# Nine score rounds for four groups of heads, with the diagonal's squares in tiles of their own, and a written list of steps

## The chip, the cores and the metric

The kernel runs on one core of one Trainium2 chip, as one launch. The metric is the device time of that launch in microseconds (us); lower is better. Five engines work side by side and are synchronised by semaphores: TensorE (PE, with its weight loads as PEld), VectorE (DVE), ScalarE (ACT), GpSimd (POOL) and SyncE (SP), which here only issues DMAs.

## The reference

Two layers, each an attention with a compressive memory and then a ReLU feed-forward, on x of 2048 tokens by 640 in bfloat16. The same weights serve both layers. The sequence is cut into N = 4 segments of L = 512 tokens; there are H = 32 heads of Dh = 20.

```python
def _A_ref(x, wq, wk, wv, wo, beta):
    q, k, v = ...                       # x @ wq, wk, wv; by head and segment
    phi = lambda t: jnp.where(t > 0, t + 1.0, jnp.exp(t))
    mask = (ar[:, None] < ar[None, :]) * -1e9
    for s in range(N):
        logits = jnp.einsum('bhqd,bhkd->bhqk', qs, ks) * scale + mask
        a_dot = jnp.einsum('bhqk,bhkd->bhqd', softmax(logits), vs)
        pq = phi(qs)
        num = jnp.einsum('bhld,bhde->bhle', pq, M)
        den = jnp.einsum('bhld,bhd->bhl', pq, z)[..., None] + 1e-06
        o = g * (num / den) + (1.0 - g) * a_dot
        pk = phi(ks)
        M = M + jnp.einsum('bhld,bhle->bhde', pk, vs)
        z = z + jnp.einsum('bhld->bhd', pk)
    return o @ wo
# twice: x = x + A(layernorm(x)); x = x + relu(layernorm(x) @ w1) @ w2
```

Attention is causal inside a segment, so of the 512 by 512 scores of a head and segment only the lower triangle counts.

## The kernel before, in words

x stays in SBUF for the whole run (`x_sb`, 16 tiles of 128 tokens). For each layer and segment the kernel normalises 512 tokens, transposes them, multiplies by wk, wq and wv, spills k and q to a DRAM scratch and reads them back into a padded layout (`pad`, four buffers, each for two groups of four heads): head hh of a group lies on the partitions 32 hh to 32 hh + 19. A score matmul therefore uses 20 rows of a 32-row strip of TensorE, and the four heads of a group run on the four strips side by side ("row tiles", 32 by 128).

**Score rounds.** `scores` (L1279 on) walks over 32 pairs of groups m (16 for each layer, four for each segment) and, for each, over the five rounds u of `ROUNDS` (L1274). An entry (z, j, o) of a round is: group z of the pair, key tile j of 128 keys, against the queries from 128 j to the end of the segment, written from column o. Key tile 0 alone is 512 columns, tiles 1 and 3 together 384 + 128, the tiles 2 of both groups 256 + 256, so each round fills 512 columns for each of four heads. A round's two halves (k = 0 and 1, two heads each) take the two score slots of PSUM, X and Y, of two banks each; in the first half of the first segment a third slot Z is lent. `exps` (L1345) runs one exponential on ScalarE for each half (L1365, 128 partitions by 1024) into `PT`, where a group has 1280 columns for each head; `causal` (L1371) zeroes the upper triangle of each 128 by 128 block on the diagonal with GpSimd (L1377). `apply` (L1385, matmuls at L1397) multiplies the probabilities by v: v's 21 columns (20 and one of ones, for the sum) are the weights, one head on each of the four 32-column strips ("quarter" or column tiles, 128 by 32), and the 512, 384, 256 and 128 queries of the four key tiles stream through in four steps. Two groups of 64 (`BY_TOKEN`) are applied the other way round (L1436). The result is evicted (L1407), transposed by DMA, divided (L1491), joined with the memory's part (`mem_read`, L1180; the memory is updated by `mem_write`, L1238), multiplied by wo and added to x (L1519); the feed-forward's second product is added at L1614, and finished tiles are stored.

**Two forms of a matmul.** `group` (L759 on) can issue each matmul of 128 by 128 weights either whole (L774, "full") or as four matmuls of 32 weight columns each on the four column tiles (L777, "quarter"), with the same result. Which is taken is decided step by step.

**What sets the order.** Every part above is a Python generator (`scores`, `exps`, `apply`, `proj_one`, `ffn`, ...) that yields operations. `Sched.run` collects the next operation of each, works out start and end from planned costs, the granted semaphores and a table of shifts (`SHIFT`), and records the best one, instruction after instruction, for every engine. A full or quarter form follows from the last form used and from how soon an apply is due (`_mode`). The engines then run these fixed programs; nothing is decided on the chip.

Of the kernel before, what the change touches and what calls it, by code (L numbers as in the profile page):

```python
# [5 lines left out]
dt = mybir.dt  # L6
# [27 lines left out]
PTH = 1280  # L34
BY_TOKEN = range(6,8)
PT_OFF = [0, 512, 1024, 896]
# [73 lines left out]
class Op:  # L110

    def __init__(self, alts, waits, dma=None, acq=None, urgent=False, take=(), mode="full", lag=0.0, port=False):
        self.lag = lag
# [8 lines left out]
        self.urgent = urgent  # L125
        self.take = take
        self.data = 0.0
# [32 lines left out]
class Spawn:  # L160
    def __init__(self, prio, gen):
        self.prio = prio
        self.gen = gen


LONE_NS = 300.0
SWITCH_NS = 96.0
COLS_LAG = 1500.0
SOFT = 400
SOFT_DMA = 1000  # L170
SOFT_FROM = ("sc",6,4,1)
SEM_NS = 60.0
PE_MARGIN = 80.0
HOLDERS = 1
SHIFT = {
# [41 lines left out]
}  # L217
HOLD_TOL = {"pe": 220.0, "act": 150.0, "dve": 200.0, "pool": 0.0, "sp": 0.0}


class Sched:


    def __init__(self, prog):
        self.P = prog
        self.free = {e: 800.0 for e in ENGS}
        self.t = {}
        self.events = {}
        self.streams = []
        self.dma_free = 0.0  # L230
        self.rank = {}
        self.mode = "full"
        self.soon = 0.0
        self.landed = set()
        self.met = {}
        self.seen = {}
        self.phase = {}
        self.made = {}
        self.held = {"dve": [], "pool": []}

    def add(self, prio, gen):
        self.streams.append([prio, gen, None, None, False])
        self.rank[id(gen)] = 0
# [8 lines left out]
    def enter(self, gen, phase):  # L252
        if self.phase.get(id(gen)) != phase:
            self.phase[id(gen)] = phase
            self.made[id(gen)] = 0

    def place(self, n, gen):
        k = self.made.get(id(gen), 0)
        return n, self.phase.get(id(gen), 0), sum(k >= x for x in (6, 20, 60))

# [6 lines left out]
    def _fill(self, st):  # L267
        while st[2] is None and not st[4]:
            try:
                y = next(st[1]) if st[3] is None else st[1].send(st[3][0])  # L270
            except StopIteration:
                st[4] = True
                return
            st[3] = None
            st[2] = y

    def _settle(self, st):

        while True:
            self._fill(st)  # L280
            if st[4]:
                return False
            y = st[2]
            if isinstance(y, (Op, Either)):
                return True
            if isinstance(y, Spawn):
                self.add(y.prio, y.gen)
                self.rank[id(y.gen)] = self.rank[id(st[1])]
                st[2], st[3] = None, (None,)
            elif isinstance(y, Need):  # L290
                if y.key not in self.events:
                    return False
                st[2], st[3] = None, (self.events[y.key],)
            else:
                s = self._pick(y.slots)
                if s is None:
                    return False
                s.free = False
                st[2], st[3] = None, (s,)
# [5 lines left out]
    def _mode(self, op):  # L305
        if op.cols is None:
            return op.mode
# [1437 lines left out]
```

## Time and profile before

| | |
|---|---|
| median of 3 runs (range) | 550.99 us (550.4 to 551.45) |
| span of the profiled execution | 549.3 us |
| the profiled execution's own time | not told apart among the three runs |
| TensorE busy | 539.8 us, 98% of the span, 9025 matmuls |
| VectorE busy | 427.8 us, 78% |
| ScalarE busy | 406.0 us, 74% |
| GpSimd busy | 195.7 us, 36% |
| exponentials (L1365) | 320, 308.9 us |
| score matmuls (L1301) | 1024, 63.4 us |

The span goes from the first to the last instruction of one profiled execution. Busy time is the time in which at least one instruction of that engine (or of that group) runs. A line number belongs to the kernel file; a line such as L774 can stand for many uses of one helper. `128*32` after a matmul's names is the size of its weights, rows by columns.

### The profile page before, as it was taken

Reading aid. Unit: us, or ns where it says so; the run is one execution under the profiler, and the core shown is the slowest. Engines: PE = TensorE matmul, PEld = TensorE weight load, DVE = VectorE, ACT = ScalarE, POOL = GpSimd, SP = SyncE. Lnnn points to the kernel's source line nnn. Section 1 sums busy time; section 2 is a strip of 40 time slices with the busy share of each in tenths; the row PEclk is TensorE's granted clock in tenths of the full one; section 3 lists DMA queues with packets and bytes.
Section 4 is the critical chain, followed back from the end, with each engine's and each line's share of the span. In section 5 each row is a group of like instructions: output and inputs, shape, how many; then the busy total and the mean of one; then the engine's idle time right before and its main releaser. Section 6 shows DMA issues by size and latency. Waiting matters only on the chain.

```text
span 549.3 us, 20483 instructions
## 1 busy us (share of the span) xinstructions
PE 539.8 (98%) x9025; PEld 305.5 (56%) x9025; DVE 427.8 (78%) x1067; ACT 406.0 (74%) x516; POOL 195.7 (36%) x305
## 2 busy tenths in 40 slices
PE   7999999999999999999999999999999999999997
PEld 6543464455554546646556555564646654757656
DVE  4899999898999989898778858997899788417102
ACT  5699899789888987788888867897778787350130
POOL 5255444333453334443433423433333333201000
PEclk9999999999999999999999999999999999999999
DMA  8699979715384175438384743336246511541201
GB/s 270 165 198 253 245 158 223 221 44 116 89 165 98 40 180 77 75 68 120 47 212 93 116 116 93 58 69 104 50 139 130 117 32 22 106 63 33 71 2 51
DMA packets 133325, 62.20 MB, mean 113 GB/s; under 512 B 112116, under 2 KB 123124, under 8 KB 133236
## 3 DMA queue, kind: packets, MB, share of 16 engines
q1 hardware_dynamic: 132672, 60.36, 51.5%
q8 instruction: 71, 1.16, 0.9%
q10 hardware_dynamic: 564, 0.53, 0.4%
q14 instruction: 18, 0.15, 0.1%
HBM read 20.56 MB, written 12.85 MB: 61 GB/s over the span
## 4 chain that ended last, share of the span: by engine, by line
PE 88%; ACT 6%; DVE 2%; DMA 2%; SPq 1%; issue 0%
PE ps L774 35%; PE ps L777 35%; PE ps L1301 8%; PE ps L1397 6%; ACT PT L1365 5%; PE ps L1180 2%; DMA x_sb<-in_A_x_dram 1%; PE ps L1572 1%; PE ps L1238 1%; DMA pad<-scr 1%; SPq L602 1%; DVE xn_tok L841 0%; SPq L612 0%; DVE stats L795 0%; DVE x_sb L1614 0%; DVE o_sb L1491 0%
## 5 line engine op out<-in xcount | busy, mean ns | idle before, releaser
L1365 ACT ACTIVATE PT<-ps 128x1024 bf16<-128x1024 f32 x320 | 308.9, 1028 | 59.3 <-PE ps L1301 57.6
L1377 POOL TENSOR_SCALAR_AFFINE_SELECT PT<-PT 128x512 bf16<-128x512 bf16 x256 | 169.3, 679 | 241.1 <-ACT PT L1365 241.0
L777 PE MATMUL ps<-xnT,w_r 128*32 128x512 bf16 x1256 | 76.0, 379 | 0.0
L777 PE MATMUL ps<-w_r,hT 128*32 128x320 bf16 (+1 forms) x1764 | 67.8, 295 | 0.0
L1614 DVE TENSOR_TENSOR x_sb<-x_sb,ps 128x320 bf16<-128x320 bf16 (+1 forms) x65 | 30.7, 474 | 43.6 <-PE ps L777 38.7
L1301 PE MATMUL ps<-pad 20*128 20x512 bf16 (+3 forms) x1024 | 63.4, 301 | 1.2 <-ACT PT L1365 0.7
L774 PE MATMUL ps<-w_r,hT 128*128 128x320 bf16 x404 | 64.2, 300 | 0.0
L795 DVE BATCH_NORM_STATS2 stats<-x_sb 128x6 f32<-128x320 bf16 x124 | 55.0, 478 | 3.8 <-DMA x_sb<-in_A_x_dram 3.0
L777 PEld LDWEIGHTS ps<-w_r,hT 128*32 128x32 bf16 x1764 | 45.2, 97 | 12.6 <-issue 1.4
L1595 ACT ACTIVATE hT<-ps 128x512 bf16<-128x512 f32 x50 | 29.9, 599 | 29.0 <-PE ps L777 25.6
L774 PE MATMUL ps<-xnT,w_r 128*128 128x512 bf16 x206 | 50.8, 380 | 0.0
L774 PEld LDWEIGHTS ps<-w_r,hT 128*128 128x128 bf16 x404 | 37.6, 98 | 19.4 <-issue 4.9
L1301 PEld LDWEIGHTS ps<-pad 20*128 20x128 bf16 x1024 | 17.9, 92 | 52.9 <-issue 24.5
L777 PEld LDWEIGHTS ps<-xnT,w_r 128*32 128x32 bf16 x1256 | 31.6, 97 | 27.8 <-issue 2.0
L1519 DVE TENSOR_TENSOR x_sb<-x_sb,ps 128x320 bf16<-128x320 bf16 x64 | 29.7, 478 | 20.4 <-PE ps L777 16.0
L811 POOL TENSOR_TENSOR rstd<-lnU,mhalf 128x2 f32<-128x2 f32 (+2 forms) x27 | 21.1, 782 | 63.5 <-DVE lnU L807 60.4
L1407 DVE CAST otu<-ps 128x512 bf16<-128x512 f32 x52 | 35.6, 685 | 9.1 <-PE ps L1397 8.2
L1397 PE MATMUL ps<-PT,v_aug 128*21 128x128 bf16 (+3 forms) x896 | 40.3, 300 | 0.0
L1594 DVE TENSOR_SCALAR hT<-ps 128x512 bf16<-128x512 f32 x54 | 36.5, 681 | 1.7 <-PE ps L774 0.7
L1491 DVE TENSOR_TENSOR o_sb<-otk,rden 128x320 bf16<-128x320 bf16 x62 | 34.8, 588 | 0.5
L981 DVE CAST stg<-ps 128x512 bf16<-128x512 f32 (+1 forms) x37 | 24.7, 669 | 12.5 <-PE ps L774 6.3
L1146 ACT ACTIVATE stg<-stg 128x512 bf16<-128x512 bf16 x50 | 31.7, 635 | 2.0 <-DVE rtmp L1144 1.8
(118 smaller groups left out, 731.5 us busy)
## 6 DMA issues: line engine op xcount, KB each, us to landing
pad<-scr SPq DMA_DIRECT2D x124, 80.0 KB
scr<-stg SPq DMA_DIRECT2D x34, 256.0 KB, 2.5
out_dram<-x_sb SPq DMA_DIRECT2D x15, 160.0 KB, 1.9
w_r<-in_B_w_dram SPq DMA_DIRECT2D x10, 216.0 KB, 4.0
w_r<-in_B_w_dram SPq DMA_DIRECT2D x13, 160.0 KB, 2.8
x_sb<-in_A_x_dram SPq DMA_DIRECT2D x10, 160.0 KB, 3.2
scr<-w_r SPq DMA_DIRECT2D x5, 256.0 KB, 4.2
wv_r<-in_A_wv_dram SPq DMA_DIRECT2D x1, 800.0 KB, 9.7
```

What stands on the lines that cost most here:

```text
L774: return e.matmul(view(dst.ap, b), a, b, start=(k == 0), stop=(k == last))
L777: return e.matmul(view(dst.ap[rows], b), part, b, start=(k == 0), stop=(k == last))
L795: tk = yield dve(320, 1, lambda e, c2=c2: e.bn_stats(stats6[:, t, c2, :], x_sb[:, t, c2 * 320:(c2 + 1) * 320]), xt)
L1146: te = yield act(512, lambda e, q=q: e.activation(q, q, ACT.Exp), [tr] + p, psum=False)
L1301: fns.append([(lambda e, z=z, j=j, hh=hh, N=N, o=o, sl=sl, q=hh % 2: e.matmul(slot.ap[:, q, o:o + N], sl.ap[32 * hh:32 * hh + DH, z, 0, 12 ...
L1365: tx = yield act(1024, lambda e, dst=dst, src=src: e.activation(dst, src, ACT.Exp, scale=SCALE), sc + pw)
L1377: tm = yield pool(600.0, lambda e, reg=reg: e.affine_select(out=reg, in_=reg, pattern=[[0, 4], [1, 128]], compare_op=ALU.is_ge, fill=0.0, ...
L1397: fns.append((lambda e, OD, j=j, hh=hh: e.matmul(OD.ap[32 * hh:32 * hh + DH + 1, 128 * j:L], VAUG[vx(a, s)][:, j, 4 * g + hh, :], pt.ap[:, ...
L1407: te = yield evac(L, 1, lambda e: e.tensor_copy(dst, OD.ap), lambda e: e.activation(dst, OD.ap, ACT.Copy), [tk] + OTU[0].tks)
L1491: to = yield dve(320, 1, lambda e, z=z, dst=dst: e.tensor_tensor(dst, av[:, z, :, :, 0:DH], rd.ap[:, z].to_broadcast([128, NJ, 4, DH]), AL ...
L1594: th = yield evac(512, 1, lambda e: e.tensor_scalar(hT[:, dc, :], bk.ap[:, :], 0.0, None, ALU.max), lambda e: e.activation(hT[:, dc, :], b ...
L1614: ta = yield dve(n, 1, lambda e: e.tensor_tensor(x_sb[:, t, c0:c0 + n], x_sb[:, t, c0:c0 + n], bk.ap[:, 0:n], ALU.add), [tk], urgent=True)
```

## The change

Three things change together.

*The layout of tokens.* In the segments 1 to 3, x is loaded so that in each odd tile the two halves of 64 tokens change places (two DMAs of 64 partitions for each pair of tiles), and stored back the same way. Segment 0 stays as it was ("plain").

*Scores and probabilities.* In the segments 1 to 3, the key tiles keep all queries that need the whole tile or its first diagonal square: the last diagonal square of 64 by 64 of each tile, four for each head, is taken out. What is left of a group fills two rounds of 512 columns (`FULLS`), so a group's part of `PT` shrinks from 1280 to 1024 columns. The squares of four groups (two pairs m, an even and the next odd one) make one ninth round in tiles of 32 rows by 64 columns, four squares for each of 16 heads. Its scores stand on 64 partitions for each key half, so it takes four exponentials (64 partitions by 1024) in place of two; they go to a new tile `DG`, of which the half that has no keys is set to zero. The apply of such a group has nine steps instead of four (`SUMS` and `DIAG`), over the same 1280 columns. In the plain segments the five rounds stay, with tile 2's probabilities in `DG`. One of the four `pad` buffers is given up for the room.

*The order.* The planner's choice is taken out. `ORDER` lists, for the whole kernel, which generator moves next, and with 80 added, that it takes its other alternative: quarter form for a matmul, VectorE in place of ScalarE for an eviction. `run` reads this list. The score rounds stay 320 halves less 24. Smaller edits: the first warming matmuls write other PSUM banks, and the last tile's three pieces are stored in halves over two queues.

```diff
-PTH = 1280
+PTH = 1024
-PT_OFF = [0, 512, 1024, 896]
+PT_OFF = [0, 512, None, 896]
+FULLS = (((0, 64, 448), (3, 384, 64)), ((2, 320, 192), (1, 256, 256), (1, 128, 64)))
+DIAG = ((0, 0, 0), (0, 3, 448), (1, 2, 256), (1, 1, 192))
+SUMS = ((0, 0, 448, 64), (3, 448, 64, 384), (2, 512, 192, 320), (1, 704, 256, 256), (1, 960, 64, 128))
...
+ORDER = """
+36 35 37*2 35 36*2 37 21 36 21 35 37 21 37 26 21 37 26*3 36 21*3 22*3 21 37 22 28 26 28 26 28 21 28 21 28 23 68 23
...
+        for word in ORDER.split():
+            code, _, count = word.partition("*")
+            for _ in range(int(count or 1)):
+                n, other = int(code) % 80, int(code) >= 80
+                st = tops[n] if n < 40 else next(x for x in self.kids[id(tops[n - 40])] if not x[3])
+                self._record(st, st[1].fn() if isinstance(st[1], Either) else st[1], other)
...
-        NPAD, NXT, NXN, NPT = 4, 2, 2, 2
+        NPAD, NXT, NXN, NPT = 3, 2, 2, 2
...
+        DG = sb("DG", [128, 2, 4, 4 * 128])
...
         ROUNDS = (((0, 0, 0),), ((0, 1, 0), (0, 3, 384)), ((0, 2, 0), (1, 2, 256)),
                   ((1, 0, 0),), ((1, 1, 0), (1, 3, 384)))
+        def plain(m):
+            return m % (NSEG * G // 2) < G // 2
+        def rounds(m):
+            return [u for u in range(5) if plain(m) or u != 2 or m % 2 == 0]
+        def turn_of(m, u):
+            if plain(m):
+                return [(z, 0, 128 * j, 128, 128 * j, L - 128 * j, o) for z, j, o in ROUNDS[u]]
+            if u == 2:
+                return [(z, 64 * (j % 2), q0, 64, q0, 64, 128 * z + 64 * y) for z in range(4) for y, j, q0 in DIAG]
+            o = [0]
+            for j, q0, nq in FULLS[u % 3]:
+                o.append(o[-1] + nq)
+            return [(u // 3, 0, 128 * j, 128, q0, nq, o[y]) for y, (j, q0, nq) in enumerate(FULLS[u % 3])]
...
-                        tx = yield act(1024, lambda e, dst=dst, src=src: e.activation(dst, src, ACT.Exp, scale=SCALE),
-                                       sc + pw)
-                        bkp.release(tx)
+                            moves = [(DG[r, t].rearrange("p z (h x) -> p h z x", h=4)[:, hs],
+                                      bkp.ap[r].rearrange("p h (z x) -> p h z x", z=4)) for t, r in enumerate(SIDES)]
+                        for dst, src in moves:
+                            tx = yield act(1024 if len(moves) == 1 else 1180, lambda e, dst=dst, src=src: e.activation(
+                                dst, src, ACT.Exp, scale=SCALE), sc + pw)
+                            ex.append(tx)
+                        bkp.release(*ex[-len(moves):])
...
+            if plain(n // 2):
+                sums = [(j, lambda hh, j=j: probs(j, hh, 128 * j, L - 128 * j), 128 * j, L - 128 * j) for j in range(NJ)]
+            else:
+                sums = [(j, lambda hh, c0=c0, nq=nq: pt.ap[:, hh, c0:c0 + nq], q0, nq) for j, c0, nq, q0 in SUMS]
+                sums += [(j, lambda hh, j=j, y=y: DG[:, j % 2, n % 4, 128 * hh + 64 * y:128 * hh + 64 * y + 64], q0, 64)
+                         for y, j, q0 in DIAG]
...
-                        S.last = yield dma(("sp", "sp", "act")[hf], dout, 256 * n, lambda e, c0=c0, n=n: e.dma_start(
-                            out[0, t * 128:(t + 1) * 128, c0:c0 + n], x_sb[:, t, c0:c0 + n]), tks)
+                        for k in range(2):
+                            S.last = yield dma(("sp", "act")[k], dout, 128 * n, lambda e, k=k, c0=c0, n=n: e.dma_start(
+                                out[0, t * 128 + 64 - 64 * k:t * 128 + 128 - 64 * k, c0:c0 + n],
+                                x_sb[64 * k:64 * k + 64, t, c0:c0 + n]), tks)
```

In `turn_of`, a part is (group, first output partition, first key, keys, first query, queries, column). A square of a key half with j odd goes to the partitions 64 to 127.

More of the change, by code (lines that the diff above doesn't have):

```diff
@@ L110, with __init__ @@
 class Op:
-    def __init__(self, alts, waits, dma=None, acq=None, urgent=False, take=(), mode="full", lag=0.0, port=False):
-        self.lag = lag
+    def __init__(self, alts, waits, dma=None, acq=None, take=(), mode="full", port=False):
         self.port = port
@@ L454, in pe, with _times @@
-def pe(ns, fns, waits=(), acq=None, take=(), mode="full", lag=0.0):
-    return Op([("pe", ns, fns, 190.0)], waits, acq=acq, take=take, mode=mode, lag=lag)
+    def _times(self, op, k, waits):
+        e, hold, fns, tail = op.alts[k]
+        m = PE_MARGIN if e == "pe" else 0.0
+        if e == "pe" and op.mode == "cols" and op.cols_ns is not None:
+            hold = op.cols_ns
+        if e == "pe" and op.mode != self.mode:
+            hold = hold + SWITCH_NS
+        start = max([self.at(t) + SEM_NS + m for t in waits], default=0.0)
+        start = max(self.free[e], start)
+        if e == "dve" and op.port:
+            for a, b in self.held["pool"][-6:]:
+                if a <= start + 66.0 < b:
+                    hold = max(hold, b - start + op.data - 70.0)
+        if e == "pool":
+            for a, b in self.held["dve"][-6:]:
+                if a < start + hold and b > start:
+                    hold = hold + b - max(a, start)
+        return start, start + hold
@@ new lines, in run @@
+    def run(self):
+        tops = list(self.streams)
+        first = tops[0]
+        self._settle_all()
+        for word in ORDER.split():
[4 more added lines that the diff above has]
+                self._record(st, st[1].fn() if isinstance(st[1], Either) else st[1], other)
+                self._settle(st)
+                self._settle_all()
+                if isinstance(first[1], Either):
+                    first[1].fn()
+        assert not self.streams
@@ new lines, in _record @@
+    def _record(self, st, op, other):
+        k = int(other and len(op.alts) > 1)
+        e, _, fns, tail = op.alts[k]
+        if op.cols is not None:
+            op.mode = "cols" if other else "full"
+            fns = op.cols if other else fns
+        waits, slot = op.waits, None
+        for s in op.take:
+            s.free = False
+        if op.acq is not None:
+            slot = self._pick(op.acq)
+            slot.free = False
+            waits = waits + slot.tks
+            fns = [(lambda eng, fn=fn, slot=slot: fn(eng, slot), mark) for fn, mark in fns]
+        start, end = self._times(op, k, waits)
+        self.P.waits(e, waits)
+        self.free[e] = end
+        if e == "pe":
+            self.mode = op.mode
+        if e == "dve" and op.port:
+            self.held[e].append((end - op.data, end))
+        elif e == "pool":
+            self.held[e].append((start, end))
+        if op.dma is not None:
+            tk = self.P.dma(e, fns[0][0], op.dma)
+            self.dma_free = max(self.dma_free, start + 300.0) + tail[1]
+            self.t[(id(tk[0]), tk[1])] = max(self.dma_free, end) + tail[0]
+            if tail[2]:
+                self.free[e] = max(end, self.dma_free)
+            out = tk
+        else:
+            marks = []
+            for fn, mark in fns:
+                tk = self.P.op(e, fn, mark)
+                if tk is not None:
+                    self.t[(id(tk[0]), tk[1])] = end + tail
+                    marks.append(tk)
+            out = marks[0] if len(marks) == 1 else (marks or None)
+        st[1], st[2] = None, ((slot, out) if slot is not None else out,)
@@ L458, in either, with pe @@
+def pe(ns, fns, waits=(), acq=None, take=(), mode="full"):
+    return Op([("pe", ns, fns, 190.0)], waits, acq=acq, take=take, mode=mode)
 def either(op, cols, ns=None):
@@ L633, in x_pieces @@
             def x_pieces(s):
-                def one(t):
-                    return lambda e: e.dma_start(x_sb[:, t, :], xs[:, t, :])
-                return [("x%d%d" % (s, i), 163840, one(4 * s + i)) for i in range(4)]
+                return [("x%d%d" % (s, i), 163840, fn) for i in range(2) for fn in pair_loads(4 * s + 2 * i)]
             def rows(name, w, src, k):
@@ L933, in proj_ln @@
             if a == 0:
-                xw = [[("x10",)]] * 2 + [[("x11",)]] * 2 if s == 1 else [[("x%d%d" % (s, i),)] for i in range(NJ)]
+                xw = [[("x10",)]] * 2 + [[("x11",)]] * 2 if s == 1 else [[("x%d%d" % (s, i // 2),)] for i in range(NJ)]
             else:
@@ L1371, in causal, with flat, mask @@
+        def flat(m):
+            b = 2 * (m % 2)
+            return DG[:, :, b:b + 2].rearrange("p t z (y q) -> p t (z y) q", y=2)
+        MK = {}
         def causal(m):
+            def mask(reg, n, base, w):
+                return pool(600.0, lambda e: e.affine_select(
+                    out=reg, in_=reg, pattern=[[0, reg.shape[1]], [1, n]], compare_op=ALU.is_ge, fill=0.0, base=base,
+                    channel_multiplier=-1), w)
             mk = [[], []]
-            for u, parts in enumerate(ROUNDS):
+            last = []
+            for u in rounds(m):
@@ L1374, in causal @@
                 ex = yield Need("ex", m, u)
[L1375 to L1383 removed]
+                z = u // 3
@@ L1609, in ffn @@
             hrest = yield Need("hR", b, s)
-            sums = [[] for _ in range(NJ)]
             def residual(i, hf, bk, tk, c0, n):
@@ L1665, in items @@
-        def items(f, count):
-            def g():
-                for n in range(count):
-                    S.enter(me, 2 * NSEG * n // count)
-                    yield from f(n)
-            me = g()
-            return me
-        for f in (scores, exps):
-            me = []
-            me.append(f(me))
-            S.add(0, me[0])
-        S.add(1, items(causal, NSEG * G))
-        S.add(1, items(apply, 2 * NSEG * G))
-        S.add(1, each(free_v))
-        S.add(1, items(turn_pair, NSEG * G))
@@ L1696, in bass_interleave_layers__memory_aug_infini_attn__dense_activation_relu__prompt_kernel, with each @@
-        S.add(5, first_sums())
-        for t in range(TT // NSEG):
-            S.add(5, first_one(t))
-        S.add(5, first_ln_b())
-        S.add(5, each(proj_ln))
-        S.add(5, proj_first())
-        S.add(5, each(proj_one(0)))
-        S.add(5, each(proj_one(1)))
-        S.add(4, each(proj_v))
-        S.add(6, each(ffn))
-        S.add(5, each(ffn_rest))
-        S.add(6, each(store))
-        S.add(7, warm_pe())
-        S.add(7, consts())
-        S.add(8, loads())
-        S.add(8, late_loads())
+        def each(f):
+            for a, s in AS:
+                yield from f(a, s)
@@ new lines, in items @@
+        def items(f, count):
+            for n in range(count):
+                yield from f(n)
+        S.add(scores())
+        S.add(exps())
+        S.add(items(causal, NSEG * G))
+        S.add(items(apply, 2 * NSEG * G))
+        S.add(each(free_v))
+        S.add(items(turn_pair, NSEG * G))
+        S.add(items(divide, NSEG * G))
+        S.add(each(turn_o))
+        S.add(each(out_proj(0)))
+        S.add(each(out_proj(1)))
+        S.add(each(ln_b(0)))
+        S.add(each(ln_b(1)))
+        S.add(each(fill))
@@ L1712, in bass_interleave_layers__memory_aug_infini_attn__dense_activation_relu__prompt_kernel @@
+        S.add(each(proj_v))
+        S.add(each(ffn))
+        S.add(each(ffn_rest))
+        S.add(each(store))
+        S.add(warm_pe())
+        S.add(consts())
+        S.add(loads())
+        S.add(late_loads())
         S.run()
```

613 lines of the change are left out of this document (306 added, 307 removed), and 41 rows, old and new, of the table SHIFT.

## The prediction

> **What bounds the kernel now.** I read the page first, then the busy time by stretch, then TensorE's order of time in one steady stretch, because the first two say that only TensorE matters and the third gives its prices.
>
> ```profile
> span 549.3 us, 20483 instructions
> PE 539.8 (98%) x9025; PEld 305.5 (56%) x9025; DVE 427.8 (78%) x1067; ACT 406.0 (74%) x516; POOL 195.7 (36%) x305
> PEclk9999999999999999999999999999999999999999
> 0.00:65.00 65.00, 59.56 (x741) 32.58 (x741) 54.25 (x143) 52.35 (x77) 32.20 (x61) 1.00 0.92 228
> 65.00:520.00 455.00, 453.96 (x7580) 255.19 (x7584) 369.47 (x917) 347.05 (x428) 163.51 (x244) 1.00 0.50 102
> 520.00:546.30 26.30, 26.28 (x712) 17.74 (x700) 3.74 (x8) 6.57 (x11) 0.00 (x0) 1.00 0.08 26
> ```
>
> The columns of the last three rows are stretch, length, then busy time of PE, weight load, VectorE, ScalarE and GpSimd, the granted clock and the DMA share. TensorE is idle for 5.44 us of the first 65, for 1.04 us of the next 455, and for nothing after that; the clock is whole throughout. So the time can fall only by less TensorE work or by the 5.4 us at the start. The span is 549.3 us and the median of the runs 550.99 us: about 1.7 us lie around the span. I work on the span and add them.
>
> **Prices on TensorE.** In these rows the first number is a start; the difference of two starts is what a piece costs, since matmuls overlap their own latency.
>
> ```profile
> 200.05 0.59 PE L774 MATMUL ps<-xnT,w_r 128*128 128x512 bf16 x2
> 200.58 0.40 PE L1301 MATMUL ps<-pad 20*128 20x384 bf16 x8
> 200.90 0.72 PE L1397 MATMUL ps<-PT,v_aug 128*21 128x512 bf16 x16
> 201.45 0.82 PE L777 MATMUL ps<-xnT,w_r 128*32 128x512 bf16 x12
> 202.10 0.34 PE L1180 MATMUL ps<-BD,phs 128*32 128x147 bf16 x12
> 202.27 1.25 PE L777 MATMUL ps<-xnT,w_r 128*32 128x512 bf16 x20
> 203.46 0.40 PE L1301 MATMUL ps<-pad 20*128 20x512 bf16 x4
> 203.78 0.99 PE L774 MATMUL ps<-w_r,hT 128*128 128x320 bf16 x6
> ...
> 147.18 0.46 PE L1238 MATMUL ps<-v_aug,phk 128*32 128x147 bf16 x32
> 147.57 0.39 PE L1301 MATMUL ps<-pad 20*128 20x512 bf16 x4
> ...
> 276.09 0.40 PE L1301 MATMUL ps<-pad 20*128 20x384 bf16 x8
> 276.42 0.72 PE L1397 MATMUL ps<-PT,v_aug 128*21 128x512 bf16 x16
> ```
>
> Twelve quarter matmuls (L777, four side by side) of 512 columns take 201.45 to 202.10: 0.217 us for four, some 0.42 ns a column. Twenty take five times that, 1.08 us; the next start comes 1.19 us later, so going from quarters to a score round costs 0.11 us. The round of one part (203.46 to 203.78) costs 0.32 us: 0.217 of columns and 0.10 to leave the row tiles. A round of two parts (276.09 to 276.42) costs 0.33: 0.01 for the second part. Two full matmuls and the way into a round take 0.53 us, which is 2 x 0.216 + 0.10: full and quarter form cost the same. An apply of 1280 columns in four steps (L1397) takes 0.55 us; 0.217 for 512 columns in one step would make 0.543 for 1280, and the three further steps bring the rest: from this and the 0.01 us of the reading, about 0.004 us a step. Three steps of 147 columns (202.10 to 202.27) take 0.17 us, 0.06 each.
>
> **Part 1, the score rounds.** Counted in the order of instructions, 160 rounds become 148: in the segments 1 to 3 of both layers, four groups (a group is four heads) took ten rounds and take nine. Eight of the nine carry 512 columns; the ninth carries 64 squares of 64 columns, on eight tiles at once if the two column halves of the array work together: 8 x 64 = 512 columns of time. That is one round's columns less, 0.217 us, in each of twelve places. Against it, parts: 16 per four groups become 20 in the full rounds (two or three in each) and 8 pairs of squares, 12 more at 0.01 = 0.12 us. Net 12 x (0.217 - 0.12) = **1.2 us less**. No row shows a 32 by 64 tile. Bounds: at best the squares' own parts cost nothing (1.0 us better, 2.2 less); at worst the column halves take turns, 16 steps of 0.037 instead of 8, 12 x 0.30 = 3.6 us dearer, 2.4 more. I take the first value because the quarter tiles, which also share rows, run four abreast, and the 32 matmuls at 147.18 start within 0.39 us, 0.10 of it the switch: 9 ns each, so that issue doesn't keep 64 squares from 0.3 us either (64 x 9 would be 0.58, but those 32 hold eight of 147 columns).
>
> **Part 2, the switches.** Changes of tile shape between neighbours on TensorE fall from 322 to 308: twelve rounds fewer (24), ten more between full and quarter form. 14 x 0.10 = **1.4 us less**.
>
> **Part 3, the apply.** For 48 of the 62 applies that work by head, four steps become nine over the same 1280 columns: 48 x 5 x 0.004 = **1.0 us more**.
>
> **Part 4, quarter form.** The list runs 678 matmuls in full form where 1359 ran, and 7328 quarter matmuls in place of 4604. By the rows above this costs nothing. In the memory update (L1238) the quarter form also skips columns: 13 full matmuls of 147 columns (0.06 us each) become quarters of 42 and 63 (0.03): **0.4 us less**.
>
> Sum of TensorE's work: -1.2 - 1.4 + 1.0 - 0.4 = **-2.0 us**, bounds -3.0 and +1.6.
>
> **Part 5, the exponentials.**
>
> ```profile
> L1365 ACT ACTIVATE PT<-ps 128x1024 bf16<-128x1024 f32 x320 | 308.9, 1028 | 59.3 <-PE ps L1301 57.6
> 201.01 1.94 ACT L1365 ACTIVATE PT<-ps 128x1024 bf16<-128x1024 f32 x2 [0.33 <-PE ps L1301]
> 33.84 26.73 ACT L1365 ACTIVATE PT<-ps 128x1024 bf16<-128x1024 f32 x29
> ```
>
> There is no gain here: a square round needs four instructions of 64 partitions by 1024 in place of two of 128 by 1024, so there are still 320, and the time goes with the 1024. Both score slots stay taken until all four are done. After a normal round that is 0.43 us (200.58 to 201.01) + 1.94; after a square round 0.43 + four at 0.92 (29 in 26.73 us) + 0.11 = 4.2 us. By the prices above, the new list puts 4.5 to 5.4 us of other TensorE work behind each of the twelve square rounds and, as before, about 2.5 us behind the others. This cover holds: cost nothing. If it went, each 0.1 us on each exponential beyond 1.1 us would cost 12 x 0.4 us.
>
> **Part 6, the start.** From 33.84 us on, ScalarE does 29 exponentials without a break: there it, not TensorE, sets the pace, and much of the 5.44 us lies in it. The first twenty rounds keep their number and form; the list puts 37.7 us of TensorE work from the first to the twentieth where 36.0 stood. Work that fills idle time there is gone later: up to 1.7 us. I take **1.0 us less**, as other waits of the start are for weights and inputs, whose loads stay in their order. x's two early pairs now come as four DMAs of half the partitions, two more issues on SP, beside the same bytes.
>
> **Part 7, everything else.** VectorE has 17 copies fewer and six maxima more, ScalarE 11 instructions more, of some 830 us busy together; GpSimd has the same number of masks of the same 512 elements. Two fills of zeros (1024 words on VectorE, one a layer) stand in front of the first squares' masks; the exponentials of the square round cover them. One of four pad buffers goes.
>
> ```profile
> 60.76 4.43 DMA pad<-scr
> PE ps L1301 <- DMA pad<-scr: 0.4, 1, 0.4
> 546.03 0.24 PE L777 MATMUL ps<-w_r,hR 128*32 128x160 bf16 x4
> 546.33 0.32 DVE L1614 TENSOR_TENSOR x_sb<-x_sb,ps 128x160 bf16<-128x160 bf16 x1 [0.65 <-PE ps L777]
> 546.68 0.38 ACTq L1642 DMA_DIRECT2D out_dram<-x_sb  x1
> out_dram<-x_sb ACTq DMA_DIRECT2D x1, 40.0 KB, 2.2
> ```
>
> TensorE waited once for a pad, 0.4 us. A pad takes 4.4 us to land and a pad serves two groups, one of 32 such pairs, so some 14 us (455 us over 32) pass from one to the next; three pads, two in use, leave a refill about 10 us: nothing. What queues behind a refill on SP are the transposes, which have the same slack. The last piece's store is halved over two queues; most of its 2.2 us is not bytes: **0.1 us less**.
>
> Total: -2.0 - 1.0 - 0.1 = -3.1; span 546.2, time 551.0 - 3.1 = **547.9 us**.
>
> **Rivals.** *Short leads (slower).* From the order I took, for each wait of TensorE on VectorE after the start, the TensorE work between the matmul that VectorE waited for and the waiting one. A quarter of these leads were under 1.9 us and are now under 1.4; the shortest twentieth go from 1.36 to 0.98.
>
> ```profile
> L1407 DVE CAST otu<-ps 128x512 bf16<-128x512 f32 x52 | 35.6, 685 | 9.1 <-PE ps L1397 8.2
> ```
>
> A bare eviction needs about 0.30 us of handing over (546.03 to 546.33 in the rows of part 7, the last matmuls' start to VectorE's) and 0.685: 1.0 us, so the shortest leads are just covered and anything queued ahead on VectorE decides. If one in ten of the 335 waits loses 0.25 us, that is 8 us: 556; it tips over 551 from 0.1 us each. Against it, most leads exceed 2 us.
>
> *Four exponentials (slower).* If reading half the partitions makes them 1.25 us apart, the hold is 0.43 + 5.0 + 0.11 = 5.5 us against 4.9 on average: 12 x 0.6 = 7 us, 555. It decides from 1.1 us on.
>
> *Squares one by one (slower).* 40 matmuls of 21 columns on the whole array take 1.03 us, 25 ns each:
>
> ```profile
> 59.24 1.18 PE L1436 MATMUL ps<-w_r,PT 128*128 128x21 bf16 x40
> 60.27 0.38 PE L774 MATMUL ps<-hT,wk_r 128*128 128x512 bf16 x1
> ```
>
> If each square costs that, whatever its tile, a square round takes 1.6 us in place of 0.3: 12 x 1.3 = 16 us, 564. The 9 ns of the 32 matmuls at 147.18 speaks against it. The Trainium skill (TensorE: Matmul & The Clock Gate, "Wait — 56ns, not 53.3ns?") has this as a rule: from one matmul's start to the next it never takes less than about 25 ns, however few the columns. On the full array the trace agrees (25 ns); between quarter tiles it doesn't (9 ns), and the measurement decides.
>
> *Halves in turn (no change).* The worse bound of part 1, +3.6: 551.5.
>
> *A better start (faster).* If the list also removes half of the 5.4 us, and the squares' parts are free: 547.9 - 1.7 - 1.0 = 545.2.
>
> That the change doesn't do what it says is excluded: 148 rounds stand in the order.
>
> **Chances.** Forecast 0.48 (its own range 546 to 549.5), better start 0.17, halves in turn 0.08, short leads 0.15, four exponentials 0.09, one by one 0.03. A change under 0.2%, 1.1 us, can't be told from none. Faster by more: 0.48 + 0.17 = 0.65; slower: 0.27, of which some 0.02 end too small to tell, 0.25; within: 0.08 and those, 0.10. The range leaves out only the far ends of the slower cases: 544.5 to 555.
>
> **What would show it.** Right: PE busy near 537 us of a span of 546; 148 rounds; a square round's start 0.4 us before the next piece; two applies' starts 0.57 us apart from what follows; PE idle after 65 us still near 1 us. Wrong: idle in front of TensorE in the middle, by VectorE (short leads) or by ScalarE behind the square rounds; exponentials on 64 partitions of more than 1.1 us; a square round of 0.7 us or 1.7 us.

## The result: slower, 568.4 us

The changed kernel takes 568.38 us (median of 4 runs, 567.8 to 568.87) where the kernel before takes 550.97 on the same chip. The ratio is 1.0315, with a 95% interval of 1.0301 to 1.0330. The forecast was 547.9, within 544.5 to 555. In the changed kernel's file the lines stand some places off those of before: L772 is the full form, L775 the quarter form, L1315 the score matmuls, L1395 the exponentials, L1479 the apply, L1233 the memory update.

The profile's page of the changed kernel, its counts and its code loads:

```profile
span 567.1 us, 28697 instructions
PE 546.5 (96%) x13117; PEld 330.1 (58%) x13117; DVE 413.9 (73%) x1058; ACT 412.7 (73%) x527; POOL 196.9 (35%) x305
PEclk9999999999989999999999999999999999999999
q8 instruction: 103, 1.69, 1.3%
```

and the same last line of the kernel before:

```profile
q8 instruction: 71, 1.16, 0.9%
```

Its columns are loads, MB, and share of the DMA engines' time. A load is 1.16 MB / 71, some 16 KB. With two instructions for a matmul (the weight load and the matmul), TensorE runs 18,050 before and 26,234 now; 71 and 103 loads of 256 instructions would be 18,176 and 26,368. So these are the blocks of 256 instructions in which TensorE's program comes in.

Busy time by stretch (length; busy PE, weight load, VectorE, ScalarE, GpSimd; clock, DMA share, GB/s):

```profile
0.00:65.00 65.00, 60.09 (x1035) 34.03 (x1036) 53.37 (x136) 54.59 (x81) 31.58 (x60) 1.00 0.81 204
65.00:535.00 470.00, 457.82 (x11330) 276.90 (x11330) 350.67 (x905) 355.10 (x442) 165.30 (x245) 1.00 0.53 102
535.00:565.00 30.00, 28.63 (x764) 19.17 (x756) 9.86 (x18) 2.99 (x5) 0.00 (x0) 1.00 0.20 49
```

After 65 us TensorE now idles for 12.2 us where it idled for 1.04, while VectorE has 13.9 us less to do over the whole span than before, ScalarE 6.7 more and GpSimd 1.2 more. The view of waits names the largest item (engine, tile, line, releaser: us in total, times, longest):

```profile
PE ps L775 <- issue: 7.6, 9, 2.3
PE ps L1479 <- POOL PT L1414: 1.5, 1, 1.5
PE ps L772 <- DVE stg L977: 1.2, 2, 0.9
PE ps L732 <- DVE beta_z L738: 1.2, 1, 1.2
PE ps L1315 <- ACT PT L1395: 0.6, 1, 0.6
PE ps L1479 <- issue: 0.6, 1, 0.6
```

"Issue" means that TensorE waited for nothing the profile shows, neither another engine nor a transfer of the kernel's. Such stops in TensorE's order of time (start, length):

```profile
71.31 0.57 PE L775 MATMUL ps<-wv_r,hT 128*32 128x320 bf16 x12
71.71 0.44 PE L775 MATMUL ps<-wo_r,oT 128*32 128x320 bf16 x7
73.99 1.11 PE L775 MATMUL ps<-wo_r,oT 128*32 128x320 bf16 x25 [1.84 <-issue]
...
159.78 0.26 PE L1233 MATMUL ps<-v_aug,phk 128*32 128x42 bf16 x12
159.85 0.32 PE L775 MATMUL ps<-wv_r,xnT 128*32 128x320 bf16 x4
162.43 0.59 PE L775 MATMUL ps<-wv_r,xnT 128*32 128x320 bf16 x12 [2.26 <-issue]
...
227.74 0.26 PE L1479 MATMUL ps<-DG,v_aug 128*21 128x64 bf16 x12
228.58 0.21 PE L1479 MATMUL ps<-DG,v_aug 128*21 128x64 bf16 x4 [0.58 <-issue]
```

In the first, the break falls after seven matmuls of a run of 32: three into a set of four quarters that share one input and wait for nothing between them. With all instructions of TensorE's compiled program numbered in order, thirteen breaks, counted from start to start 9.3 us in all, stand at instruction 200 or 201 of a block of 256. Four others without a releaser (0.83 us before 93.49, 0.31 before 244.23, under 0.3 before 260.85 and 384.10) stand elsewhere and are counted with the other waits. The kernel before has at most one such break, of 0.1 us.

The trace also has the time of each load, and this ties the breaks to the loads directly. Twelve of the thirteen end 1.2 to 1.6 us after a load has landed, the other (0.18 us, before 158.16) 2.1 us after one. The break that ends at 162.43 waits for a load that started at 159.36 and landed at 161.13. When loads and blocks are counted side by side, instruction 200 of a block never starts sooner than 1.2 us after its load has landed; in the kernel before the least is 1.9 us.

Of the wrong signs named ahead, two fit in part: some of the idle in front of TensorE is VectorE's, and a square round takes 0.64 us, near the 0.7. The largest item was named by none.

Adding up starts of matmuls against the prediction's prices, the 17.8 us of the span come out so (a wait counted from start to start is some 0.2 us longer than the idle time that the views give, since a matmul overlaps its own latency):

| | before | after | difference |
|---|---|---|---|
| TensorE's work by the prices, a square round as measured | 535.7 | 536.5 | +0.8 |
| waits before 65 us | 7.1 | 5.5 | -1.6 |
| breaks at instruction 200 or 201 of a block of 256 | 0.1 | 9.3 | +9.2 |
| other waits after 65 us, a slow clock among them (1.7, below) | 1.2 | 10.0 | +8.8 |
| behind the last matmul's start | 3.3 | 3.7 | +0.4 |

The rows sum to 17.6; the other 0.2 is rounding and pieces under 0.06 us each.

### The profile page after: what moved, and what is told of

It is laid out like the page before. It is cut to its first block, busy times and chain, and to the rows that moved or that the text cites. A ratio compares the mean times of both kernels' runs of the same rounds, so it can differ in the third digit from the quotient of the medians.

```text
span 567.1 us, 28697 instructions
## 1 busy us (share of the span) xinstructions
PE 546.5 (96%) x13117; PEld 330.1 (58%) x13117; DVE 413.9 (73%) x1058; ACT 412.7 (73%) x527; POOL 196.9 (35%) x305
## 4 chain that ended last, share of the span: by engine, by line
PE 80%; DVE 11%; DMA 3%; issue 2%; POOL 2%; SPq 1%; ACT 0%; DVEq 0%; ACTq 0%
PE ps L775 48%; PE ps L772 17%; PE ps L1315 8%; PE ps L1479 5%; DMA otk<-otu 2%; DVE xn_tok L839 2%; PE ps L1175 2%; DMA x_sb<-in_A_x_dram 1%; DVE stats L793 1%; POOL rstd L809 1%; DVE hT L1677 1%; DVE phs L1142 1%; PE ps L1655 1%; DVE rtmp L1139 1%; DVE o_sb L1574 1%
## 5 line engine op out<-in xcount | busy, mean ns | idle before, releaser
L1395 ACT ACTIVATE PT<-ps 128x1024 bf16<-128x1024 f32 x256 | 248.5, 1024 | 46.5 <-PE ps L1315 45.2
L1414 POOL TENSOR_SCALAR_AFFINE_SELECT PT<-PT 128x512 bf16<-128x512 bf16 (+1 forms) x144 | 97.5, 698 | 184.9 <-ACT PT L1395 184.9
L775 PE MATMUL ps<-w_r,hT 128*32 128x320 bf16 (+1 forms) x2968 | 126.8, 297 | 1.1 <-issue 1.1
L775 PE MATMUL ps<-xnT,w_r 128*32 128x512 bf16 x1728 | 110.8, 381 | 1.8 <-issue 1.2
L1414 POOL TENSOR_SCALAR_AFFINE_SELECT DG<-DG 128x512 bf16<-128x512 bf16 x112 | 72.8, 686 | 56.3 <-ACT DG L1395 56.3
L775 PEld LDWEIGHTS ps<-w_r,hT 128*32 128x32 bf16 x2968 | 76.3, 97 | 24.4 <-issue 4.2
L1395 ACT ACTIVATE DG<-ps 64x1024 bf16<-64x1024 f32 (+1 forms) x64 | 64.4, 1020 | 10.9 <-PE ps L1315 9.9
L775 PEld LDWEIGHTS ps<-xnT,w_r 128*32 128x32 bf16 x1728 | 43.0, 97 | 39.3 <-issue 5.4
L1315 PE MATMUL ps<-pad 20*64 20x64 bf16 (+5 forms) x1984 | 62.7, 238 | 0.8 <-ACT PT L1395 0.6
L1315 PEld LDWEIGHTS ps<-pad 20*128 20x128 bf16 (+1 forms) x1984 | 27.0, 96 | 45.8 <-issue 16.1
L775 PE MATMUL ps<-wo_r,oT 128*32 128x320 bf16 x856 | 45.2, 300 | 2.3 <-issue 2.0
L839 DVE TENSOR_SCALAR xn_tok<-x_sb,mv,rstd 128x640 bf16<-128x640 bf16 x60 | 32.1, 553 | 6.2 <-POOL rstd L809 5.1
L1479 PE MATMUL ps<-PT,v_aug 128*21 128x64 bf16 (+6 forms) x1056 | 35.3, 257 | 0.4 <-DVE hT L1677 0.4
```

Source lines behind the costliest of these rows:

```text
L775: return e.matmul(view(dst.ap[rows], b), part, b, start=(k == 0), stop=(k == last))
L839: nm = lambda e, bx, t, k: e.tensor_scalar(bx.ap[:, k * D:k * D + D], x_sb[:, t + k, :], mv[:, t + k, 0:1], rstd[:, t + k:t + k + 1], ALU. ...
L1315: fns.append([(lambda e, z=z % 2, p=p, k0=k0, nk=nk, q0=q0, nq=nq, o=o, hh=hh, sl=pads[m + z // 2], q=hh % 2: e.matmul(slot.ap[p:p + nk, q ...
L1395: tx = yield act(1024 if len(moves) == 1 else 1180, lambda e, dst=dst, src=src: e.activation(dst, src, ACT.Exp, scale=SCALE), sc + pw)
L1414: return pool(600.0, lambda e: e.affine_select(out=reg, in_=reg, pattern=[[0, reg.shape[1]], [1, n]], compare_op=ALU.is_ge, fill=0.0, base ...
L1479: fns.append((lambda e, OD, y=y, j=j, src=src, q0=q0, nq=nq, hh=hh: e.matmul(OD.ap[32 * hh:32 * hh + DH + 1, q0:q0 + nq], VAUG[vx(a, s)][: ...
```

## Experiments

**Theory.** The quarter form issues four weight loads and four matmuls where the full form issues one of each. Where quarters and squares stand close, TensorE uses up 256 instructions faster than the next block comes in, and stops. **Rival:** the new list leaves TensorE's waits for VectorE too little lead (the prediction's short leads), and the breaks are a part of that.

**1. The changed kernel with fewer quarters.** Its order of steps is kept; runs of matmuls between two score rounds that may be issued either way go in full form.

```diff
+    def reform(self):
+        for n, (_, _, mode, whole) in enumerate(self.form):
+            if whole is not None:
+                run.append(n)
+                continue
+            if left in ("rows", "halves") and mode in ("rows", "halves"):
+                free.update(run)
+            run, left = [], mode
...
+            for fn, mark in whole:
+                new.append(("op", fn, sem[0][2] if mark else None, sem[0][3] if mark else 0))
```

> The changed kernel with its order untouched; only the form differs: wherever all steps between two score rounds can take either form, they are issued as full matmuls instead of four quarters. 10783 matmuls instead of 13117, TensorE's columns and changes of shape the same to 1 us. Code theory (TensorE's program comes in loads of 256 instructions, and dense stretches use one up before the next is there): loads fall from 103 to about 85, TensorE's stops at the same place of every 256 instructions, 9.6 us in the changed kernel, fall under 3 us, and the clock stays whole: 557 to 560 us. Short leads, or the new rounds, as the cause: nothing moves, 567 to 569 us.

559.42 us (558.78 to 559.9), ratio 1.0149 [1.0134, 1.0164]: 9.0 us less than the changed kernel, from the form alone. Its page and its waits:

```profile
span 557.0 us, 24029 instructions
PE 542.4 (97%) x10783; PEld 322.9 (58%) x10783; DVE 416.2 (75%) x1058; ACT 412.3 (74%) x527; POOL 196.6 (35%) x305
PEclk9999999999999999999999999999999999999999
q8 instruction: 84, 1.38, 1.0%
...
PE ps L802 <- DVE stg L1007: 2.3, 3, 1.2
PE ps L1509 <- POOL PT L1444: 1.6, 1, 1.6
PE ps L1685 <- issue: 1.4, 1, 1.4
...
PE ps L1345 <- issue: 0.3, 1, 0.3
```

84 loads, and of the thirteen breaks the view still has two: one at L1685, which exists in quarter form only, and one of 0.3 us at a score round. Both stand at instruction 200 or 201 of their block and end 1.2 to 1.3 us after a load has landed. The slice with a lower clock is gone too.

**2. The kernel before with more quarters.** The planner's order stays; every matmul that may be quartered is.

```diff
-                if op.mode == "cols" and op.cols is not None:
+                if op.cols is not None:
```

> The kernel before with its order untouched; every matmul that can take either form is issued as four quarters: 13420 matmuls instead of 9025, the same columns, 8 changes of shape more (0.8 us), 0.4 us less in the memory update. Code theory: 105 loads instead of 71, stops appear at one place of every 256 instructions, 554 to 561 us. Short leads or the new rounds as the cause: the form costs nothing, 550.5 to 552 us.

560.14 us (558.31 to 561.55), ratio 1.0160 [1.0131, 1.0190]: 9.1 us dearer, with neither new rounds nor a new list. Its page, the first of its waits, and its longest break:

```profile
q8 instruction: 105, 1.72, 1.3%
...
PE ps L777 <- issue: 5.0, 3, 3.0
...
10.71 0.40 PE L777 MATMUL ps<-xnT,wq_r 128*32 128x128 bf16 x15
14.10 0.28 PE L777 MATMUL ps<-xnT,wq_r 128*32 128x128 bf16 x5 [2.99 <-issue]
```

Again a set of four is cut (15 = 4 + 4 + 4 + 3). The three longest breaks, 3.0, 1.3 and 1.1 us, stand at instruction 200 or 201 of their block and end 1.4 to 1.5 us after a load has landed; counted from start to start, breaks at this place come to 6.2 us. A fourth without a releaser, 0.7 us before 176.34, stands elsewhere. The other waits after 65 us rise from 1.2 to 3.7. Runs 1 and 2 take the cause away and put it in, and the time follows both ways: TensorE stops for its own instructions.

How closely the instructions stand is not all that decides, though. In the traces of the two kernels and of runs 1 and 2, the median load starts 0.3 to 0.5 us after TensorE has come to instruction 200 of the block ahead, and takes 1.0 to 1.1 us. A block of the changed kernel that is used up in 3.5 us (442.58 to 446.07) then costs no stop. Ahead of the break that ends at 69.24 the load started 3.9 us after that instruction, and a block that lasted 5.5 us was too short; ahead of the three breaks of run 2 it was 2.9 to 3.6 us, and the blocks lasted 3.2, 5.0 and 4.4 us. While those three loads were late, the DMA engines' mean busy share was 1.08, 1.00 and 0.88. Whether the kernel's own transfers hold the loads up, so that moving transfers would help as fewer quarters do, was not tried.

**3 and 4. The new rounds without the list.** Run 3 puts them and the new layout under the planner of before and its table of shifts. Run 4 does so with an empty table, beside the kernel before with an empty table.

```diff
-PTH = 1280
+PTH = 1024
+FULLS = (((0, 64, 448), (3, 384, 64)), ((2, 320, 192), (1, 256, 256), (1, 128, 64)))
...
-SHIFT = {
-    (0, 5, 1): -12, (0, 6, 1): -12, (1, 0, 0): -200, (1, 0, 2): -75, (1, 1, 0): -100, (1, 1, 1): 875, (1, 1, 2): 1112,
...
+SHIFT = {}
```

> The new layout and the nine rounds, with the kernel before's planner and its table of shifts in place of the written list: 10999 matmuls, 299 changes of shape. Counted with a square round of 0.64 us, as the changed kernel's trace shows it, TensorE's work is 2.4 us more than before. Code theory: few stops, 551 to 557 us. Rounds as the cause of most of the 17.4 us: 563 us or more. Short leads as the cause (this planner keeps a margin): 551 to 554 us.

590.74 us (588.8 to 592.51): a miss, and of little use. The table's shifts belong to other steps; TensorE waits for transposes (L798, 8.0 us) and for exponentials.

> The nine rounds and the new layout with the planner of before and an empty table of shifts; to be read against the next run, which has the five rounds under the same empty table. The rounds cost TensorE's work alone (+0.9 us by count with a square round of 0.64 us): within 5 us of the next run. Rounds that bring waits of their own (four exponentials, masks for four groups at once): 15 us or more above it.

> The kernel before with an empty table of shifts (and the first probability buffer held until the warming matmuls are done): 8308 matmuls, no code stops. 555 to 580 us; what counts is the distance to the run before it.

570.77 us (569.09 to 574.02) against 563.84 (563.58 to 564.45), 6.9 us more, between the two expectations. In the waits of the first and then of the second:

```profile
PE ps L1296 <- ACT DG L1378: 4.1, 3, 2.6
...
PE ps L1260 <- ACT PT L1324: 4.7, 4, 2.0
```

Under this planner TensorE waits for the exponentials of a square round at three places. What that costs isn't settled: all waits for exponentials of scores (`DG` and `PT`) are 6.6 us against 4.7, and the two profiled executions also differ in their granted clock, 0.988 against 0.994. The waits of the changed kernel name none for `DG`. So these runs don't part the new rounds from the new list.

**5. VectorE relieved.** In the kernel of run 1, and as a control in the kernel before, the 124 statistics instructions read 32 of 320 columns (0.176 us in place of 0.474, 18.7 us busy in place of 55.7; most of the statistics' input is left out).

```diff
-                    stats6[:, t, c2, :], x_sb[:, t, c2 * 320:(c2 + 1) * 320]), xt)
+                    stats6[:, t, c2, :], x_sb[:, t, c2 * 320:c2 * 320 + 32]), xt)
```

> The kernel of the full form (559.4 us), where the statistics of the layer norm are taken over 32 of every 320 columns, so its output is not the reference's: 124 instructions on VectorE shrink from 0.48 us to about 0.17, some 38 us of its 416, and nothing else moves. Its TensorE still stops for 7.0 us after the first 65 us, away from the code places, where before stops for 1.2. Short leads theory (VectorE, queued up, is late for TensorE): most of that goes, 553 to 556 us. If the stops have another cause (masks, exponentials, DMAs): 558 to 560 us.

> The kernel before with the same short statistics (its output is not the reference's either), as the control: it stops for 1.2 us after the first 65 us, so little is to be had; the start's waits may shorten by 1 to 2 us. Short leads theory and its rival: 548.5 to 551 us.

557.79 us (556.73 to 559.13) and 549.9 (548.78 to 552.14). Against each other that is a ratio of 1.0139 / 0.999 = 1.015, as in run 1: 37 us less work on VectorE do not close the gap. 557.79 lies between that run's two expectations, nearer to the one for other causes. Most waits stand at the same instructions as in run 1; the longest of its late ones, 1.2 us for `stg`, is gone, and one of 0.9 us without a releaser has come just behind it.

**6. Six instructions of VectorE put behind the eviction that follows them.** At the waits that are left in run 1, an eviction does stand behind something else. One of three places where this is the mask product `BD`, VectorE and then TensorE:

```profile
194.62 0.90 DVE L1293 TENSOR_TENSOR BD<-M_sb,maskg 128x294 bf16<-128x294 f32 x1
195.44 0.68 DVE L1707 TENSOR_SCALAR hT<-ps 128x512 bf16<-128x512 f32 x1
...
195.17 0.60 PE L802 MATMUL ps<-xnT,wq_r 128*128 128x512 bf16 x2
196.18 0.82 PE L802 MATMUL ps<-xnT,wq_r 128*128 128x512 bf16 x3 [0.40 <-DVE hT L1707]
```

```diff
+MOVES = ((4130, 4142), (3567, 3570), (2379, 2381), (2182, 2187), (1851, 1857), (852, 853))
...
+        for a, b in MOVES:
+            steps.insert(b, steps.pop(a))
```

> Full-form kernel of the first experiment (559.4 us, ratio 1.0149) with six instructions of VectorE put behind the one or two evictions that followed them, and nothing else changed: three products BD (0.90 us each at 86.8, 194.6 and 442.2 us), one xn_tok (0.77 at 229.96), one rden (0.61 at 250.6) and one phs (0.41 at 380.45). If TensorE's late waits come from an eviction that stands in VectorE's queue behind something that nobody waits for yet, these six places lose 0.82 + 0.57 + 0.47 + 0.48 + 0.54 + 0.34 = 3.2 us of waiting at most: 556.2 to 557.4, ratio 1.009 to 1.011. If the leads are bare, shorter than the eviction itself, or the wait moves to the next eviction, little comes of it: 558.7 to 559.9, ratio 1.0135 to 1.0160.

Nothing was gained. Five runs gave 558.52, 559.66 and three times 562.1 to 562.3, median 562.09, ratio 1.0199 [1.0177, 1.0221]; the profile is of the shortest, and no profile tells what the longer ones wait for. In the profiled one the span is 556.8 us (557.0 in run 1) and the late waits sum to 6.8 us (7.0). The same place:

```profile
193.78 0.68 DVE L1712 TENSOR_SCALAR hT<-ps 128x512 bf16<-128x512 f32 x1
194.38 0.91 DVE L1298 TENSOR_TENSOR BD<-M_sb,maskg 128x294 bf16<-128x294 f32 x1
...
196.16 0.48 DVE L1066 CAST v_aug<-ps 128x320 bf16<-128x320 f32 x1
...
195.85 0.38 PE L807 MATMUL ps<-xnT,w_r 128*128 128x512 bf16 x1
196.70 0.31 PE L807 MATMUL ps<-wv_r,xnT 128*128 128x320 bf16 x1 [0.46 <-DVE v_aug L1066]
...
382.75 0.59 PE L807 MATMUL ps<-xnT,w_r 128*128 128x512 bf16 x2
384.38 0.60 PE L807 MATMUL ps<-xnT,wq_r 128*128 128x512 bf16 x2 [1.03 <-DMA xnT<-xn_tok]
```

The wait for `hT` is gone and one for `v_aug`, which now stands behind the same product, has come six matmuls, some 1.3 us, later. Counted from start to start, at the six places 4.1 us of waiting became 2.6, and a new wait for a transpose took 1.2 back. So at this place the swap passes the wait on, and the six together hardly shorten the sum; that the leads in this order are short for VectorE as a whole would explain it, but isn't shown.

**7. Squares of half the columns.** The kernel of run 1, with 32 columns streamed through each square (half of the squares' scores is left out).

```diff
-                return [(z, 64 * (j % 2), q0, 64, q0, 64, 128 * z + 64 * y) for z in range(4) for y, j, q0 in DIAG]
+                return [(z, 64 * (j % 2), q0, 64, q0, 32, 128 * z + 64 * y) for z in range(4) for y, j, q0 in DIAG]
```

> Full-form kernel of the first experiment, whose 64 squares of a square round stream 32 of their 64 columns; half of the squares' scores is left out. One profile, for the time from the first to the last square's start, 0.497 us in the changed kernel (7.8 ns a square). If the two column halves take turns and the columns set the pace, it falls to about 0.26 to 0.30 us. If issue sets it (64 weight loads and 64 matmuls), it stays at 0.45 to 0.50.

A square round of the changed kernel, and below it one of this run (one profile, span 558.6 us):

```profile
158.16 0.70 PE L1315 MATMUL ps<-pad 20*64 20x64 bf16 x64 [0.18 <-issue]
158.79 0.59 PE L775 MATMUL ps<-wv_r,xnT 128*32 128x320 bf16 x12
...
155.69 0.68 PE L1345 MATMUL ps<-pad 20*64 20x32 bf16 x64
156.29 0.59 PE L805 MATMUL ps<-wv_r,xnT 128*32 128x320 bf16 x12
```

0.63 us to the next start becomes 0.60; less the 0.10 of the switch, 0.53 and 0.50. From the first to the last square's start, the quantity forecast, it is 0.497 and 0.483 us in the rounds without a break. Half the columns save 0.01 to 0.03 us. So the columns don't set the pace, whether the column halves take turns or not; something that comes with each square does, 0.50 us / 64 = 7.8 ns a square. Each square brings a weight load and a matmul, and each tile takes eight squares in turn; which of these it is, no run tells.

## Why the prediction was wrong

**Part 4 failed: "By the rows above this costs nothing."** The price of a step was right: TensorE's counted work in run 1 is 535.3 us, 1.2 from the changed kernel's, with 3112 quarter matmuls fewer. What it left out is that a quarter step is eight instructions and a full one two. TensorE has 8184 more instructions, 32 more blocks: 4344 of them come from the form, and 3840 from parts 1 and 3, whose squares, further parts and further steps are 1920 more matmuls. At the price of 0.217 us for four quarters of 512 columns, 256 instructions last 32 x 0.217 = 6.9 us; at 320 columns (0.136), 4.3; a square round spends 128 in 0.54. The page of before showed the 71 loads, and I did not read that line as a resource. Run 1 puts the form at 9.0 us, the 1.7 us of a slow clock among them, and run 2, from the other side, at 9.1. Of the Trainium skill, "Runtime: NRT & Kernel Launch", section "Instruction fetch mechanics", says that a sequencer fetches its next 16 KiB while it runs the present ones and that crossing to them is mostly hidden. The kernel before agrees (0.1 us over 71 blocks); the changed kernel doesn't (9.3 us over 103).

**Part 1 was mis-sized.** A square round takes 0.54 + 0.10 us, not 0.30 + 0.10: 12 x 0.24 = 2.9 us, which eats the 1.2 gained and the 1.4 of part 2. The row of 32 matmuls in 0.39 us that I set against it spoke for it, since it gave 9 ns a matmul and 64 x 9 = 0.58; I put that aside. It comes within 0.1 us of *halves in turn*, for another reason than that rival's.

**Parts 3 and 5 held.** Nine steps of an apply, in quarter company on either side:

```profile
236.13 0.61 PE L1479 MATMUL ps<-PT,v_aug 128*21 128x448 bf16 x20
236.57 0.29 PE L1479 MATMUL ps<-DG,v_aug 128*21 128x64 bf16 x16
236.69 0.58 PE L775 MATMUL ps<-w_r,hT 128*32 128x320 bf16 x12
```

take 0.56 us, where four took 0.55. And a square round's exponentials, by shape:

```profile
L1395 ACT ACTIVATE DG<-ps 64x1024 bf16<-64x1024 f32 x48 | 48.9, 1018 | 10.3 <-PE ps L1315 9.4
```

take 1.02 us each, below the 1.1 from which *four exponentials* would have decided. Behind the written list that rival falls; under the untuned planner (run 4) TensorE did wait 4.1 us for `DG`, though it waited less for `PT` there.

**Part 6** was right in kind: the start's waits fell by 1.6 us, forecast 1.0; by the busy time of the first 65 us, which the prediction went by, the idle fell only from 5.44 to 4.91 us. **Part 7's** tail rose by 0.4 us in place of falling by 0.1. *Squares one by one* (1.6 us a round) falls.

**Short leads**, to which I gave 0.15, is the other half. With the blocks' share taken off (run 1), the kernel is still 8.4 us behind. Its late waits are 7.0 us against 1.2 (as idle time in the views, 4.7 against 1.2; of the 4.7, 3.1 end with VectorE, 1.0 with ScalarE, 0.5 with a DMA); the longer of the two breaks left adds 1.5, pieces under 0.06 us add 1.7, and the counted work (0.4 less) and the start (0.7 less) give back. That most leads exceed 2 us, my point against it, was no defence, since the loss lies in some sixteen places. Run 5 shows that it isn't the amount of VectorE's work and run 6 that these six swaps don't mend it. That this half is the list's, and not the new rounds', is argued from the names in the waits (mostly evictions, none for `DG`), not shown, since runs 3 and 4 didn't part the two; which steps of the list would have to move is open too.

No experiment points to a version faster than the kernel before: the squares save TensorE nothing, and before hardly waits for its blocks.

## What to carry over

Count instructions beside columns: where a form of equal time needs four times the instructions, look at how long 256 of them last in the densest stretch and at how busy the DMA engines are there, and read the line of code loads as a resource. Here, waits "issue" that cut a set of matmuls with nothing between them, at the same place of a block and just behind a load's landing, were that and not a dependence. And an order in which the bounding engine hardly waits is itself part of the time: here the kernel with the new list waits 5.8 us more in some sixteen places, more than the new rounds were to bring.

## What the runs showed of the hardware

A break costs up to 2.3 us in the changed kernel and 3.0 in run 2, not a fixed price for each load; most loads cost nothing. One long break, the one behind 159.85, was followed by a slower clock:

```profile
159.80:162.50 2.70, 0.44 (x27) 0.21 (x20) 0.81 (x2) 2.62 (x4) 0.00 (x0) 1.00 1.13 66
162.50:167.50 5.00, 5.00 (x84) 3.07 (x87) 2.96 (x9) 1.19 (x2) 1.27 (x2) 0.66 0.18 44
167.50:180.00 12.50, 12.50 (x220) 6.25 (x213) 11.13 (x30) 11.02 (x14) 7.48 (x11) 1.00 0.48 119
```

The granted clock is 0.66 for the 5 us behind it, 5 x 0.34 = 1.7 us more; it is 0.50 from 163.4 to 166.8. Behind the break of 1.84 us that ended at 73.99, and behind the longest of all, the 2.99 us of run 2 that ended at 14.10 (second row), it stayed whole:

```profile
74.00:79.00 5.00, 5.00 (x137) 3.97 (x140) 3.83 (x10) 2.63 (x4) 3.15 (x5) 1.00 0.65 224
...
14.20:19.20 5.00, 5.00 (x150) 3.99 (x151) 3.04 (x8) 1.81 (x5) 0.00 (x0) 1.00 0.17 40
```

So the length of a break alone doesn't decide it. What does wasn't tried.
